# Later places in VectorE's queue for the reciprocals and x's multiplications of a linear-attention and gated-MLP kernel

## The chip, the cores and the metric

The kernel runs on one core of a Trainium2 chip. The metric is the device time of one execution in microseconds (us). A profiled execution is a single one, with its own time.

## The reference

Eight batches of eight heads (pairs of heads: 32 in all), 576 tokens each, head size 64, 128 features. In outline:

```python
proj = q_or_k @ w_phi; proj = proj - max(abs(proj))      # phi
phi = concat(exp(proj), exp(-proj))
kv = einsum('bhsf,bhsd->bhfd', k_p, v); z = sum(k_p, axis=2)
num = einsum('bhsf,bhfd->bhsd', q_p, kv)
den = einsum('bhsf,bhf->bhs', q_p, z) + 1e-06
x = (num / den) laid out as 4608 tokens x 512
out = ((x @ w_a) * (x @ w_b)) @ w_out                     # 512 -> 1536 -> 512
```

## The kernel before

**Two kinds of work side by side.** The first 630 us or so hold the attention of the 32 pairs and, interleaved with it, the first pass of the MLP over 9 blocks of 512 tokens (`moe_block`, one third of the 1536 hidden columns). After that come two more passes of the MLP over all tokens, in a form with fewer products (`later_passes`, `winograd`); no line of the change lies there. Operands are split in a high and a low part, so that most products are three matmuls.

**The steps of one pair.** `k_load` fetches and splits k and v; `features` (lines 216 to 246) projects k in two chunks of 256 tokens (`c0` = 0 and 2), and VectorE takes the largest magnitude (`m`, line 229) and subtracts it (`kd`, line 230), so each pair has two `kd` of this size; ScalarE then takes both exponentials, and VectorE makes the low part `kel`. `k_finish` makes `kvh` and `kvl`. `q_side` does the same for q and leaves unnormalized columns in `xun` and the denominators in `den`, both in DRAM (lines 381 and 382).

**Reciprocals.** `reciprocals` (lines 385 to 393) reads the denominators of a pair back as 128 rows of 9 (`r<-den`, line 389), VectorE adds EPS (line 390) and takes the reciprocal (line 391), and the result goes to `rec` in DRAM (line 392).

**x.** `x_chunk` (lines 562 to 579) loads 128 rows of `xun` (one pair's columns) for a block of 512 tokens, broadcasts that pair's `rec` over them (`rb<-rec`, line 576), and VectorE multiplies (line 578). `load_x` splits the product in `xh` and `xl` (lines 152 and 157). A block has four such chunks, c = 0 to 3, one for each pair of a batch, and every sum of line 621 needs all four. There are 36 multiplications in all. When block j is made, the last batch that it needs is `((j + 1) * 512 - 1) // 576`.

**What sets the order.** `attention_steps` lays out the steps of the pairs in turns: pair i begins at turn 5i for the first seven pairs and 4 turns apart after that, its reciprocals are at turn 13 of the pair, and the block that a finished batch allows is put into the work queue 8 turns later (`BLOCK_LAG`); the queue gives off 0.6 or 0.62 of a step in each turn. This is the order in which the program is traced. The order in each engine's queue is another one: line 1124 asks the framework to arrange every engine's queue at compile time by its own estimate of when each operand is ready, and an instruction that the estimate has ready early may be queued ahead of work that was traced before it. On the chip, each queue is then worked off in that order; an instruction that waits holds up what is queued behind it. All DMAs are issued from one queue, SyncE's (SP).

Of the kernel before, what the change touches and what calls it, by code (L numbers as in the profile page):

```python
# [13 lines left out]
ALU = mybir.AluOpType  # L14
# [4 lines left out]
P = 128  # L19
EPS = 1e-6  # L20


TURNS0, TURNS, PAIRS0 = 5, 4, 7
# [7 lines left out]
Q_TURNS, Q_STEP, QB, PB, Q32 = (4, 6, 10), 3, 2, 2, 2  # L31
# [29 lines left out]
def tile_kernel(ctx, tc, qT, km, kr, vm, vr, w_phi, w_a, w_b, w_out, out):  # L61
# [13 lines left out]
    nc = tc.nc  # L75
    B, H, _, S = qT.shape
    NPAIR = H // 2
    D, F = w_phi.shape
# [29 lines left out]
    def products(a, b):  # L108

        if len(a) == 1:  # L110
            return [(a[0], b[0])]
        return [(a[0], b[0]), (a[0], b[1]), (a[1], b[0])]
# [32 lines left out]
    def engine(step, b):  # L145
        return {"v": nc.vector, "s": nc.scalar}[ENGINES[step][min(b, 2)]]
# [7 lines left out]
    def split(hi, lo, src, eng_hi, eng_lo):  # L154

        copy(eng_hi, hi, src)
        eng_lo.tensor_tensor(lo, src, hi, op=ALU.subtract)  # L157

    def stack(hi_lo, src, eng_hi, eng_lo):

        copy(eng_hi, hi_lo, src)
        eng_lo.tensor_tensor(hi_lo[D:], src[D:], hi_lo[D:], op=ALU.subtract)

    def k_load(b, pr, a1, a2, ps, consts, st):
        vaug = consts[-1]
        u = f"{b}_{pr}"
        i = b * NPAIR + pr
        n = NFULL * P
        k32 = a1.tile([P, n], F32, tag="k32", bufs=2, name=f"k32_{u}")
        nc.sync.dma_start(k32, km[b, pr])  # L170
        if i < PLAIN_KV:
            v32 = a1.tile([P, NFULL, 2, D + 1], F32, tag="vl", bufs=2, name=f"v32_{u}")
            nc.vector.memset(v32[:, :, :, D : D + 1], 1.0)
        else:
            v32 = a1.tile([P, NFULL, 2, D], F32, tag="v32", name=f"v32_{u}")
        nc.sync.dma_start(v32[:, :, :, :D], vm[b, pr])
        yield
        st["k", b, pr] = (k32,)
        if i >= PLAIN_K:
            kh, kl = (a1.tile([P, n], F32R, tag=f"k{p}", bufs=2, name=f"k{p}_{u}") for p in "hl")  # L180
            split(kh, kl, k32, engine("k_hi", b), engine("k_lo", b))
            st["k", b, pr] = (kh, kl)
        yield
        st["v", b, pr] = (v32,)
        if i >= PLAIN_KV:
            va = vaug[pr % 2]
            vl = a1.tile([P, NFULL, 2, D + 1], F32R, tag="vl", bufs=2, name=f"vl_{u}")
            split(va[:, :, :, :D], vl[:, :, :, :D], v32, engine("v_hi", b), engine("v_lo", b))
            st["v", b, pr] = (va, vl)
        yield  # L190
# [25 lines left out]
    def features(u, i, k_, c0, n, a2, ps, consts):  # L216

        wk32, wks = consts[3:5]
        d = a2.tile([P, 4, F], F32, tag="kd", bufs=2, name=f"kd_{u}")[:, : 2 * n]
        pk = ps.tile([P, 2, 2 * F], F32, tag="att", name=f"pk_{u}")  # L220
        parts = products(k_, (wk32,) if len(k_) == 1 else wks)
        for c in range(n):
            tok = slice((c0 + c) * P, (c0 + c + 1) * P)
            for n_, (x_, w_) in enumerate(parts):
                at = dict(start=(c == n_ == 0), stop=(n_ == len(parts) - 1))
                nc.tensor.matmul(pk[:, c], x_[:, tok], w_, skip_group_check=True, **at)
        p = pk[:, :n].rearrange("p c (j f) -> p (c j) f", j=2)
        m = a2.tile([P, 4], F32, tag="m", name=f"m_{u}")
        nc.vector.tensor_reduce(out=m[:, : 2 * n], in_=p, op=ALU.max, axis=AX.X, apply_absolute_value=True)
        nc.vector.tensor_tensor(d, p, m[:, : 2 * n].unsqueeze(2).broadcast_to([P, 2 * n, F]), op=ALU.subtract)  # L230
        yield
        plain = i < PLAIN_KV
        shape = [P, 2 * n, 2, F]
        if plain:
            e = a2.tile(shape, F32, tag=f"keh{n}", bufs=n, name=f"ke_{u}")
        else:
            e = a2.tile([P, 4, 2, F], F32, tag="ke", bufs=2, name=f"ke_{u}")[:, : 2 * n]
        nc.scalar.activation(e[:, :, 0, :], d, AF.Exp)  # L238
        nc.scalar.activation(e[:, :, 1, :], d, AF.Exp, scale=-1.0)
        es = (e,)  # L240
        if not plain:
            eh = a2.tile(shape, F32R, tag=f"keh{n}", bufs=n, name=f"keh_{u}")
            el = a2.tile(shape, F32R, tag=f"kel{n}", bufs=n, name=f"kel_{u}")
            split(eh, el, e, engine("ke_hi", i // NPAIR), nc.vector)
            es = (eh, el)
        yield es
# [16 lines left out]
    def rest_chunk(b, g, a1, a2, ps, consts, st):  # L263

        gen = features(f"{b}_{g}_r", b * NPAIR + 2 * g, st["rk", b, g], 0, 1, a2, ps, consts)
        yield next(gen)
        st["re", b, g] = next(gen)
        yield
# [116 lines left out]
    def reciprocals(b, pr, a1):  # L385
        n = 2 * S // P
        hs = slice(2 * pr, 2 * pr + 2)
        r = a1.tile([P, n], F32, tag="rec", bufs=2, name=f"r_{b}_{pr}")
        nc.sync.dma_start(r, den[b][hs].rearrange("h (a n) -> (h a) n", n=n))
        nc.vector.tensor_scalar_add(r, r, EPS)  # L390
        nc.vector.reciprocal(r, r)
        nc.sync.dma_start(rec[b][hs].rearrange("h (a n) -> (h a) n", n=n), r)
        yield

    def attention_steps(pools, consts, st):

        stages, x_first = [], first_block_x()

        def plan(unit, turns):
            for t in turns:  # L400
                stages.append((t, len(stages), unit))

        for i in range(B * NPAIR):
            b, pr = divmod(i, NPAIR)
            t0 = TURNS0 * min(i, PAIRS0) + TURNS * max(i - PAIRS0, 0)
            plan(k_load(b, pr, *pools, consts, st), [t0 + t for t in LOAD_TURNS])
            if pr % 2 == 0:
                plan(rest_load(b, pr // 2, *pools, consts, st), [t0 + t for t in REST_LOAD_TURNS])
            for c0 in range(0, NFULL, 2):
                plan(k_chunks(b, pr, c0, *pools, consts, st), [t0 + K_STEP * c0 // 2 + t for t in K_TURNS])  # L410
            if pr % 2 == 0:
                plan(rest_chunk(b, pr // 2, *pools, consts, st), [t0 + t for t in REST_TURNS])
            plan(rest_add(b, pr, st), [t0 + REST_ADD_TURNS[pr % 2]])
            plan(k_finish(b, pr, *pools, consts, st), [t0 + t for t in KV_TURNS])
            plan(q_project(b, pr, *pools, consts, st), [t0 + t for t in PROJECT_TURNS])
            for j in range(2):
                plan(q_side(b, pr, j, *pools, consts, st), [t0 + Q_STEP * j + t for t in Q_TURNS])
            plan(reciprocals(b, pr, pools[0]), [t0 + Q_STEP + Q_TURNS[-1]])
            if b == 0:
                plan(x_first, [t0 + Q_STEP + Q_TURNS[-1] + X_LAG])  # L420
            if pr == NPAIR - 1:
                plan(b, [t0 + Q_STEP + Q_TURNS[-1]])
        stages.sort(key=lambda x: x[:2])
        for turn, group in itertools.groupby(stages, key=lambda x: x[0]):
            ready = None
            for _, _, unit in group:
                if isinstance(unit, int):
                    ready = unit
                else:
                    next(unit, None)  # L430
            yield turn, ready
# [130 lines left out]
    def x_chunk(j, c, pool):  # L562

        T, u = TS[0], f"0_{j}"
        x32 = pool.tile([P, T], F32, tag="x32", bufs=NCC, name=f"x32_{u}_{c}")
        rb = pool.tile([P, T], F32, tag="rb", bufs=2, name=f"rb_{u}_{c}")

        t = j * T
        while t < (j + 1) * T:
            b, s0 = divmod(t, S)  # L570
            n = min(S - s0, (j + 1) * T - t)
            src, dst = slice(s0, s0 + n), slice(t - j * T, t - j * T + n)
            nc.sync.dma_start(x32[:, dst], xun[b][c * P : (c + 1) * P, src])
            for i in range(2):
                h = 2 * c + i
                nc.sync.dma_start(rb[i * D : (i + 1) * D, dst], rec[b][h : h + 1, src].broadcast_to([D, n]))
            t += n
        nc.vector.tensor_tensor(x32, x32, rb, op=ALU.mult)  # L578
        return x32

    def load_x(j, pool):
# [6 lines left out]
    def first_block_x():  # L588

        for x_ in load_x(0, xpool):  # L590
            first_x.append(x_)
            yield
# [404 lines left out]
    with ExitStack() as c:  # L997
        pools = attention_pools(c)
# [129 lines left out]
```

## Time and profile before

| | |
|---|---|
| median of 3 runs | 1244.07 us (1243.14 to 1244.48) |
| the profiled execution, its own time | 1244.96 us |
| its span from first to last instruction | 1243.2 us |
| PE busy | 1190.3 us (96%), x6237 |
| PE weight loads | 985.4 us (79%) |
| VectorE (DVE) busy | 1043.5 us (84%) |
| ScalarE (ACT) busy | 726.4 us (58%) |
| mean granted clock of TensorE | 0.990 |

The span is 1.8 us shorter than the execution's own time. PE is TensorE's matmuls, DVE is VectorE, ACT is ScalarE, POOL is GpSimd. Ends of matmuls are modelled, so small pauses between them are inside the busy time. [...]

### The profile page before, as it was taken

The page shows a single profiled execution, that of the slowest core. Times are in us where ns is not written, and L with a number is a line of the kernel's source. Part 1 is how long each engine was busy: PE and PEld are TensorE (multiplying, and loading weights), DVE is VectorE, ACT ScalarE, POOL GpSimd, SP SyncE. Part 2 cuts the span into 40 slices and gives each one's busy share as a digit, 9 for nine tenths or more (in the row PEclk, how much of TensorE's full clock was granted, in tenths as well). Part 3 has the DMA queues.
Part 4 walks back from the last instruction along what each step waited for, and adds up shares of the span by engine and source line. Part 5 has one row for each costly group of instructions (what it writes and reads, how often), then busy time and mean ns, then how long its engine had stood idle before and what let it go on. Part 6 is the DMA issues. An engine that isn't in the chain of part 4 may idle for free.

```text
span 1243.2 us, 18172 instructions
## 1 busy us (share of the span) xinstructions
PE 1190.3 (96%) x6237; PEld 985.4 (79%) x6237; DVE 1043.5 (84%) x1742; ACT 726.4 (58%) x1376; POOL 154.3 (12%) x68
## 2 busy tenths in 40 slices
PE   7979989999999999999999999999999999999998
PEld 4546778888888887888778888888888888888887
DVE  7989969998989899898589866889888688888686
ACT  5677778878888878788444443344444243434332
POOL 3321313222123133132100000000000000000000
PEclk9989999999999999999999999999999999999999
DMA  6764344353544445343283331647489714242312
GB/s 197 197 200 130 110 132 125 111 160 111 157 134 138 145 119 150 115 127 104 76 262 109 119 109 45 223 167 245 154 293 392 251 53 152 69 153 68 127 62 92
DMA packets 130173, 182.84 MB, mean 147 GB/s; under 512 B 35936, under 2 KB 64992, under 8 KB 130080
## 3 DMA queue, kind: packets, MB, share of 16 engines
q1 hardware_dynamic: 130080, 181.67, 46.5%
q8 instruction: 49, 0.80, 0.3%
q14 instruction: 44, 0.36, 0.1%
HBM read 123.06 MB, written 58.56 MB: 146 GB/s over the span
## 4 chain that ended last, share of the span: by engine, by line
PE 40%; DVE 7%; DMA 3%; ACT 1%; issue 1%; SPq 0%; DVEq 0%; ACTq 0%
PE po L928 7%; PE pba L716 7%; PE paa L716 7%; PE pac L716 3%; PE poa L821 3%; PE pbc L716 3%; PE po L642 3%; PE pab L716 2%; PE pb L621 2%; PE pbb L716 2%; PE pa L621 2%; DVE o L825 1%; DMA x<-xnorm 1%; DVE hl_s L157 1%; DVE top L777 1%
## 5 line engine op out<-in xcount | busy, mean ns | idle before, releaser
L359 POOL PARTITION_ALL_REDUCE mb<-p x64 | 154.2, 2437 | 439.8 <-ACT p L350 325.5
L157 DVE TENSOR_TENSOR qel<-qe,qeh 128x1152 fp32r<-128x1152 f32 x54 | 75.8, 1405 | 3.1 <-ACT qeh L150 3.0
L363 ACT ACTIVATE qe<-p 128x576 f32<-128x576 f32 x64 | 43.9, 687 | 45.2 <-DVE p L360 41.6
L578 DVE TENSOR_TENSOR x<-x,rb 128x512 f32<-128x512 f32 x36 | 31.3, 869 | 40.7 <-DMA rb<-rec 35.9
L157 DVE TENSOR_TENSOR kel<-ke,keh 128x1024 fp32r<-128x1024 f32 x50 | 62.3, 1246 | 3.7 <-ACT keh L150 3.5
L621 PE MATMUL pa<-xh,w_a_h 128*128 128x512 f32 x144 | 58.4, 405 | 6.5 <-DVE xh L152 4.9
L150 ACT CAST qeh<-qe 128x1152 fp32r<-128x1152 f32 x54 | 63.0, 1166 | 0.0
L642 PE MATMUL po<-hh,w_o_h 128*128 128x512 f32 x144 | 57.4, 408 | 5.5 <-DVE h L626 4.5
L621 PE MATMUL pb<-xh,w_b_h 128*128 128x512 f32 x144 | 58.4, 406 | 3.8 <-ACT h L625 1.4
L621 PE MATMUL pa<-xl,w_a_h 128*128 128x512 f32 x144 | 57.8, 401 | 4.2 <-DVE xl L157 4.2
L282 PE MATMUL kvps<-keh,vaug 128*65 128x256 f32 x200 | 56.3, 282 | 2.8 <-DVE kvl L312 2.8
L238 ACT ACTIVATE ke<-kd 128x512 f32<-128x512 f32 x64 | 40.8, 637 | 29.9 <-DVE kd L230 28.3
L642 PE MATMUL po<-hl,w_o_h 128*128 128x512 f32 x144 | 58.0, 404 | 0.0
L621 PE MATMUL pb<-xl,w_b_h 128*128 128x512 f32 x144 | 57.9, 402 | 0.0
L642 PE MATMUL po<-hh,w_o_l 128*128 128x512 f32 x144 | 57.7, 402 | 0.0
L621 PE MATMUL pb<-xh,w_b_l 128*128 128x512 f32 x144 | 57.6, 400 | 0.0
L621 PE MATMUL pa<-xh,w_a_l 128*128 128x512 f32 x144 | 57.3, 398 | 0.0
L928 PE MATMUL po<-hl,w_o_h 128*128 128x512 f32 x144 | 56.4, 392 | 0.3 <-DVE hl L157 0.3
L928 PE MATMUL po<-hh,w_o_l 128*128 128x512 f32 x144 | 56.1, 389 | 0.0
L282 PE MATMUL kvps<-keh,vl 128*64 128x256 f32 x200 | 55.8, 279 | 0.0
L282 PE MATMUL kvps<-kel,vaug 128*65 128x256 f32 x200 | 55.8, 279 | 0.0
L150 ACT CAST keh<-ke 128x1024 fp32r<-128x1024 f32 x50 | 52.5, 1049 | 4.2 <-PE kvps L282 4.0
(338 smaller groups left out, 3877.1 us busy)
## 6 DMA issues: line engine op xcount, KB each, us to landing
x<-xnorm SPq DMA_DIRECT2D x32, 512.0 KB
o<-part SPq DMA_DIRECT2D x61, 256.0 KB
q<-in_qT SPq DMA_DIRECT2D x108, 144.0 KB
xun<-xn SPq DMA_DIRECT2D x64, 144.0 KB
xnorm<-x SPq DMA_DIRECT2D x36, 256.0 KB
part<-o SPq DMA_DIRECT2D x18, 512.0 KB
part<-o SPq DMA_DIRECT2D x36, 256.0 KB
k<-in_km SPq DMA_DIRECT2D x32, 256.0 KB
```

The source lines that it names most:

```text
L150: eng.copy(dst, src)
L157: eng_lo.tensor_tensor(lo, src, hi, op=ALU.subtract)
L238: nc.scalar.activation(e[:, :, 0, :], d, AF.Exp)
L282: nc.tensor.matmul(st["kv_ps", b, pr][:width, j], v_[:, j, :width], e_[:, j], start=(left == NFULL and j == 0 and n_ == 0), stop=(left == ...
L359: nc.gpsimd.partition_all_reduce(mb, p32, P, bass_isa.ReduceOp.absmax)
L363: nc.scalar.activation(e[:, 0], p32, AF.Exp)
L578: nc.vector.tensor_tensor(x32, x32, rb, op=ALU.mult)
L621: nc.tensor.matmul(acc, w[:, cc * P : (cc + 1) * P], x, start=(k == 0), stop=(k == 3 * NCC - 1))
L642: nc.tensor.matmul(acc, w[:, cc * P : (cc + 1) * P], h, start=(k == 0), stop=(k == 3 * NFS[p] - 1))
L716: nc.tensor.matmul(accs[to][i], w_, x_, skip_group_check=True, **at)
L821: nc.tensor.matmul(accs[to][m], w_, x_, skip_group_check=True, **flags)
L928: nc.tensor.matmul(acc[key], w[:, cc * P : (cc + 1) * P], h[:, tok], skip_group_check=True, **n_)
```

## The change

A dictionary keeps, for each pair, the two `kd` instructions of line 230. The add of a pair from the eighth on (i >= 7) is queued on VectorE behind the second `kd` of the pair three later; x's multiplication of such a pair is queued behind the first `kd` of the pair four later. `tc.issue_after` fixes the order within one engine's queue and adds no wait. Where that pair does not exist (the last batch), the multiplication is kept behind the VectorE instruction traced just before it (`tc.keep_in_program_order`); the adds of the last three pairs get no such place. The add, the reciprocal and the store of `rec` are traced two turns after the load of the denominators instead of in the same turn, for all pairs.

```diff
+    behind = {}
+
+    def placed(i, c0, op):
+
+        if i >= PAIRS0 and (i + c0[0], c0[1]) in behind:
+            with tc.issue_after(behind[i + c0[0], c0[1]]):
+                return op()
+        return op()
+
@@ features
-        nc.vector.tensor_tensor(d, p, m[:, : 2 * n].unsqueeze(2).broadcast_to([P, 2 * n, F]), op=ALU.subtract)
+        kd = nc.vector.tensor_tensor(d, p, m[:, : 2 * n].unsqueeze(2).broadcast_to([P, 2 * n, F]), op=ALU.subtract)
+        if n == 2:
+            behind[i, c0] = kd.ins
@@ reciprocals
         nc.sync.dma_start(r, den[b][hs].rearrange("h (a n) -> (h a) n", n=n))
-        nc.vector.tensor_scalar_add(r, r, EPS)
+        yield
+        placed(b * NPAIR + pr, (3, 2), lambda: nc.vector.tensor_scalar_add(r, r, EPS))
         nc.vector.reciprocal(r, r)
@@ attention_steps
-            plan(reciprocals(b, pr, pools[0]), [t0 + Q_STEP + Q_TURNS[-1]])
+            plan(reciprocals(b, pr, pools[0]), [t0 + Q_STEP + Q_TURNS[-1] + t for t in (0, 2)])
@@ x_chunk
-        nc.vector.tensor_tensor(x32, x32, rb, op=ALU.mult)
+        multiply = lambda: nc.vector.tensor_tensor(x32, x32, rb, op=ALU.mult)
+        pair = ((j + 1) * T - 1) // S * NPAIR + c
+        if pair + 4 < B * NPAIR:
+            placed(pair, (4, 0), multiply)
+        else:
+            tc.keep_in_program_order(multiply())
```

## Rows read from the trace of the kernel before

**Rows 1.** Busy time by stretch: us from:to, length, busy us of each engine, granted clock.

```profile
180.00:190.00 10.00, 7.42 (x33) 5.94 (x32) 6.46 (x11) 4.84 (x11) 0.20 (x1) 0.83 0.34 105
...
490.00:505.00 15.00, 11.65 (x60) 9.54 (x59) 12.79 (x18) 11.92 (x25) 5.15 (x2) 0.89 0.53 167
...
616.00:626.00 10.00, 6.97 (x17) 5.19 (x18) 5.74 (x13) 1.67 (x3) 0.00 (x0) 0.66 0.64 188
626.00:650.00 24.00, 22.59 (x96) 17.59 (x95) 21.84 (x50) 12.80 (x29) 0.00 (x0) 1.00 0.84 275
sum 490.00, PE 469.07 PEld 404.88 DVE 425.58 ACT 378.72 POOL 108.98; mean PE 46.91 PEld 40.49 DVE 42.56 ACT 37.87 POOL 10.90
```

**Rows 2.** PE's waits, 160 to 632 us: total us, times, longest us.

```profile
PE pa L621 <- DVE xl L157: 4.2, 3, 2.6
PE pa L621 <- DVE xh L152: 4.0, 4, 2.6
PE po L642 <- DVE h L626: 3.0, 1, 3.0
PE kvps L282 <- DVE kvl L312: 2.8, 3, 1.3
```

**Rows 3.** Line 578, 160 to 600 us: VectorE's idle time before it (us, times).

```profile
  DMA rb<-rec: 20.9, 14
```

**Rows 4.** Line 390, 160 to 600 us, the same columns.

```profile
  DMA r<-den: 10.7, 9
```

**Rows 5.** VectorE's timeline at the end of the attention: start us, us, instruction, [idle before].

```profile
609.01 0.22 DVE L391 RECIPROCAL r<-r 128x9 f32<-128x9 f32 x1
...
614.68 0.69 DVE L578 TENSOR_TENSOR x<-x,rb 128x512 f32<-128x512 f32 x1 [4.90 <-DMA rb<-rec]
...
618.23 0.68 DVE L626 TENSOR_TENSOR h<-pb,h 128x512 f32<-128x512 f32 x1
```

**Rows 6.** VectorE's timeline: second kd of pair 19, first kd of pair 20.

```profile
354.12 0.68 DVE L230 TENSOR_TENSOR kd<-pk,m 128x512 f32<-128x512 f32 x1
...
360.64 0.68 DVE L230 TENSOR_TENSOR kd<-pk,m 128x512 f32<-128x512 f32 x1
```

**Rows 7.** SyncE's queue, 160 to 600 us: waits, total us, times, longest us.

```profile
SPq L392 <- DVE r L391: 29.1, 18, 3.0
```

**Rows 8.** VectorE's timeline, blocks 1 to 6: chunk 3's multiplication, then first kd four pairs later.

```profile
183.47 0.69 DVE L578 TENSOR_TENSOR x<-x,rb 128x512 f32<-128x512 f32 x1 [4.75 <-DMA rb<-rec]
...
196.01 0.68 DVE L230 TENSOR_TENSOR kd<-pk,m 128x512 f32<-128x512 f32 x1
...
266.06 1.31 DVE L578 TENSOR_TENSOR x<-x,rb 128x512 f32<-128x512 f32 x1 [1.06 <-DMA rb<-rec]
...
272.86 0.69 DVE L230 TENSOR_TENSOR kd<-pk,m 128x512 f32<-128x512 f32 x1
...
341.18 0.81 DVE L578 TENSOR_TENSOR x<-x,rb 128x512 f32<-128x512 f32 x1 [0.92 <-DMA rb<-rec]
...
344.22 0.68 DVE L230 TENSOR_TENSOR kd<-pk,m 128x512 f32<-128x512 f32 x1
...
414.02 0.69 DVE L578 TENSOR_TENSOR x<-x,rb 128x512 f32<-128x512 f32 x1 [1.02 <-DMA rb<-rec]
...
425.03 0.68 DVE L230 TENSOR_TENSOR kd<-pk,m 128x512 f32<-128x512 f32 x1
...
492.83 0.69 DVE L578 TENSOR_TENSOR x<-x,rb 128x512 f32<-128x512 f32 x1 [0.68 <-DMA rb<-rec]
...
494.88 0.68 DVE L230 TENSOR_TENSOR kd<-pk,m 128x512 f32<-128x512 f32 x1
...
567.43 0.69 DVE L578 TENSOR_TENSOR x<-x,rb 128x512 f32<-128x512 f32 x1 [1.50 <-DMA rb<-rec]
...
577.49 0.68 DVE L230 TENSOR_TENSOR kd<-pk,m 128x512 f32<-128x512 f32 x1
```

**Rows 9.** The chain of waits in order of time: start us, us, what.

```profile
631.43 2.80 PE pa L621 x12
```

## The prediction

> **What bounds the kernel now.** I read the profile in this order. First the busy times by stretch, from 160 us (about where the places of the change begin to act) to 650 us (the end of the attention): PE is busy 469.1 of 490 us, DVE 425.6 [rows 1]. So PE has about 21 us of visible pauses here, and no more than these, with what a lower clock costs, can be won while PE's work stays the same; after 650 us the change has nothing. Second, PE's own waits from 160 to 632 us [rows 2]: nearly all of the time stands against DVE, and most of it against two of its products, xh and xl of line 621 (8.2 us in seven waits), a single wait of 3.0 us for h, and three for kvl (2.8 us). Third, what DVE itself waited for in these places: in 160 to 600 us it stood 20.9 us at x's multiplication until the broadcast of rec had landed [rows 3] and 10.7 us at the add until the denominators had [rows 4], 31.6 us together. While it stands, the steps that make PE's operands are queued behind the waiting instruction.
>
> The granted clock ties the two together. Three stretches lie below full clock: 180 to 190 us at 0.83, 490 to 505 us at 0.89, 616 to 626 us at 0.66 [rows 1]. Each holds one of the three long PE stops: 2.6 us for xh, 2.6 us for xl, 3.0 us for h [rows 2]. In the first, the multiplication of block 1's last chunk started at 183.47 us after DVE had stood 4.75 us [rows 8]. In the last, DVE stood 4.90 us before a multiplication at 614.68 us, and h, which PE needed, came behind it at 618.23 us [rows 5]. [...]
>
> **The change part by part.** The sum is made against the profiled execution's 1244.96 us, which is 0.9 us above the median of the runs.
>
> *No instruction is added.* The counts of DVE, PE and DMA instructions stay. The new order edges lie within DVE's queue, so there is no new semaphore wait; they cost nothing by themselves.
>
> *Adds and reciprocals behind the second kd three pairs later, multiplications behind the first kd four pairs later.* The data then has at least the distance between these two kd to come: the tightest that I found from pair 7 on is 354.12 to 360.64 us, 6.5 us [rows 6]. A reciprocal at 609.01 us was followed by its multiplication at 614.68 us [rows 5], 5.7 us for the store, the broadcast and the wait in SP's queue. 6.5 is above 5.7, so the waits of rows 3 and 4 should nearly vanish. The SP queue: the store of rec holds SP until the reciprocal is done, 29.1 us in 18 waits [rows 7]. The store and the broadcasts move with the reciprocal, so SP waits for it neither more nor less as long as the arranged order moves too; behind them stand loads of k, v and q, which are issued some turns ahead of their use. I take 0.
>
> What PE gets back:
> - the end: block 7's and 8's multiplications are pinned behind what was traced before them, so h of block 6 no longer stands behind them. The stop of 3.0 us goes, and the clock with it: 10 us at 0.66 lose 3.4 us. 6.4 us.
> - block 1: 2.6 us, and 10 us at 0.83, 1.7 us. 4.3 us.
> - block 5: 2.6 us, and 15 us at 0.89, 1.65 us. 4.25 us.
> - the other five waits for xh and xl: 8.2 - 5.2 = 3.0 us.
> - kvl: it is merely late in DVE's queue. Between 0 and 2.8 us; I take the middle, 1.4, since only some of these waits have a DVE stop close ahead of them.
>
> Together 19.35 us.
>
> What it costs. The last chunk of a block now comes later, and no sum of line 621 can end without it. Work passed over, less the multiplication's own wait that goes, is kd start - multiplication start - wait [rows 8]: block 1: 12.54 - 4.75 = 7.79; block 2: 6.80 - 1.06 = 5.74; block 3: 3.04 - 0.92 = 2.12; block 4: 11.01 - 1.02 = 9.99; block 5: 2.05 - 0.68 = 1.37; block 6: 10.06 - 1.50 = 8.56. Sum 35.6 us, in which PE has only attention and the three earlier chunks. Lower end: 0, attention fills it all (it is ready sooner when DVE does not stand). Upper end: the MLP's whole share of PE is lost. Twelve matmuls of 512 columns take 2.80 us [rows 9], so a block's 144 take 33.6 us; from pair 11's kd at 196.01 to pair 27's at 494.88 us [rows 8] are four batches, 74.7 us each; share 0.45, 16.0 us. I take 8.2 us, because the nearest row is what waiting for xh and xl costs at these same starts today [rows 2]: the next late operand is again the last chunk's xh and xl, only at another place in the queue.
>
> *Pinned multiplications of block 8.* Its four multiplications of 0.69 us, 2.8 us in all, move from gaps to just ahead of their casts, where DVE is busy 21.84 of 24 us [rows 1]. Between 0 and 2.8 us; I take 1.0, nearer to 0, as the 48 output matmuls of block 7 (11.2 us at the pace of rows 9) stand on PE meanwhile. Below 0 there is nothing: they gain no time by going later.
>
> *The two turns for the first seven pairs and the last three*, which get no place. The add there may be queued a little later or earlier. I take 0, with two mean waits of rows 4 (10.7 / 9 = 1.2 us) to either side, 2.4 us.
>
> Sum: -19.35 + 8.2 + 1.0 = -10.15 us. 1244.96 - 10.15 = 1234.8 us; less the 0.9 us by which the profiled execution lies over the median, **1234 us**. With the bounds: all costs at 0, kvl whole and 2.4 us to the good, 1244.07 - 20.75 - 2.4 = 1221 us; all costs at their upper ends, kvl at 0, 1244.07 - 17.95 + 16.0 + 2.8 + 2.4 = 1247 us. About what can be told from no change in this kernel is 0.2%, 2.5 us.
>
> **The rivals.**
>
> *DVE is the bound, and all that it waited comes off.* For it: it is busy 425.6 of 490 us and stood another 31.6 us in 160 to 600 us [rows 3, 4], so it had little left. Against it: PE has only 21 us of visible pauses to give [rows 1], and its work does not shrink. It would give 1244.07 - 31.6 = 1212 us. [...] Chance 0.08.
>
> *Slower: the blocks starve PE.* The place is chunk 3 of blocks 1 to 6. The first kd four pairs later is a worse place than the wait was: the stops for xh and xl do not go, they move with the chunk. Then the gains left are the end and kvl, 6.4 + 1.4 = 7.8 us, less 1.0 for block 8. It turns where more than 6.8 us of the 35.6, 19%, finds no attention work. At 0.35 of it, 12.5 us, the time is 1244.07 - 6.8 + 12.5 = 1250 us; at the full 0.45 and with two starts at the lower clock (1.7 us each, as now) 1257 us. For it: the operands of attention come from the same DVE, 87% busy, and block 4's and block 6's chunks come 10.0 and 8.6 us later. Against it: today's starts are waited for too, and cost 8.2 us in all. Chance 0.20.
>
> *No change that can be told.* Two ways lead here. The places fix an order, not a distance: if attention quickens and the two kd come closer than the 5.7 us of the chain, part of the waits returns. Or the whole order of PE is arranged anew and small pauses open elsewhere, by as much as the waits give back. 1242 to 1246 us. Chance 0.16.
>
> **How the numbers follow.** The forecast has 0.56, the rivals 0.08, 0.20 and 0.16. Faster by over 0.2%: forecast and the first rival, 0.64. Within: 0.16. Slower: 0.20. The forecast's own range is 1227 to 1241 us. The range of 8 in 10 runs from 1222 us, where nearly all of the gain comes at no cost, to 1248 us, the forecast's upper bound and the nearer part of the slower rival; left out are the first rival and the farther part of the second.
>
> **What would show it.** In the profile after: DVE's idle time before lines 578 and 390 in 160 to 600 us falls from 31.6 us to under 6 us; the stretch around the end of block 6 has no stop for h and no clock below 1; PE's waits for xh and xl stand near 8 us, without a stop above 2 us; chunk 3's multiplications come right behind a kd. If idle time before these lines stays over 15 us, the spacing was misjudged. If it goes and the time does not fall, PE's waits will show it: a sum for xh and xl above 15 us is the slower rival; PE pauses gone and the attention's end 25 us or more earlier would be the first.

## The result and the profile after

The changed kernel takes 1227.59 us (median of 4 runs, 1223.45 to 1227.88), the kernel before 1244.28 us beside it (4 runs). The ratio, which is formed from all runs and not from the two medians, is 0.9855, with a 95% interval of 0.9829 to 0.9881. In the medians it is 16.7 us, 1.3%, faster. The forecast was 10.15 us faster, 1234 us; 1227.59 us lies at the lower edge of its own range of 1227 to 1241 us. The profiled execution after took 1227.31 us, its span is 1225.4 us, 17.8 us shorter than before.

The order of reading is that of the prediction. First the busy times by stretch of the changed kernel (columns as in [rows 1]), the three stretches that had lain below full clock and then 160 to 630 us:

```profile
180.00:190.00 10.00, 10.00 (x74) 9.16 (x72) 8.97 (x17) 9.67 (x21) 3.73 (x2) 1.00 0.44 129
...
490.00:505.00 15.00, 14.53 (x87) 12.19 (x86) 12.22 (x18) 13.41 (x25) 4.26 (x2) 1.00 0.37 99
...
616.00:626.00 10.00, 10.00 (x43) 8.07 (x44) 9.43 (x21) 4.76 (x11) 0.00 (x0) 1.00 1.08 335
```

```profile
160.00:630.00 470.00, 461.61 (x2838) 401.89 (x2837) 414.71 (x645) 376.79 (x720) 104.83 (x46) 1.00 0.47 137
```

and the same stretch of the kernel before:

```profile
160.00:630.00 470.00, 450.48 (x2748) 390.52 (x2747) 406.10 (x616) 367.87 (x702) 108.98 (x45) 0.99 0.44 131
```

PE's pauses in this stretch went from 19.5 us to 8.4 us, 11.1 us less, and 90 more matmuls fit in. The three stretches with a granted clock of 0.83, 0.89 and 0.66, which lost 1.7, 1.65 and 3.4 us by an estimate from [rows 1] (length times what the clock lacks of 1), are at full clock, 1.00. 11.1 + 6.75 = 17.9 us is as much as the whole difference, in the stretch and of the kind that the prediction named.

The row of 180 to 190 us flatters, though: block 1's stop did not go, it moved behind this row. A wider stretch shows it, in the kernel before, in the changed one, and in a kernel with the changed one's queues (x from pair 8, below):

```profile
180.00:215.00 35.00, 32.42 (x187) 27.76 (x186) 30.67 (x47) 27.12 (x53) 9.41 (x4) 0.95 0.41 122
```

```profile
180.00:215.00 35.00, 30.37 (x213) 26.55 (x211) 33.78 (x51) 29.97 (x59) 9.61 (x4) 1.00 0.47 135
```

```profile
180.00:215.00 35.00, 31.53 (x212) 27.60 (x211) 33.91 (x52) 30.09 (x59) 9.62 (x4) 0.95 0.44 123
```

PE pauses 2.6 us there in the kernel before and 4.6 us in the changed one, and in the repetition the lower clock is back as well, 0.95 as in the kernel before. What was won in pauses lies behind it: 215 to 630 us has 14.9 us of them before and 1.7 us after.

A second look at the same sum is the end of the MLP's first pass on PE, the last matmul with the 512 columns of block 8 before the first of the second pass. In the kernel before and in the changed one (timeline of PE: start us, us, instruction):

```profile
700.18 0.39 PE L642 MATMUL po<-hh,w_o_l 128*128 128x512 f32 x1
```

```profile
681.16 0.40 PE L659 MATMUL po<-hh,w_o_l 128*128 128x512 f32 x1
```

19.0 us earlier; what follows takes 1225.4 - 681.2 = 544.2 us instead of 1243.2 - 700.2 = 543.0 us, 1.2 us more. That 17.9 us meets the difference of the spans, 17.8 us, is in part chance, because this execution of the changed kernel was already 1.9 us behind before 160 us (first kd of pair 9, before and after):

```profile
155.31 0.68 DVE L230 TENSOR_TENSOR kd<-pk,m 128x512 f32<-128x512 f32 x1
```

```profile
157.16 0.68 DVE L239 TENSOR_TENSOR kd<-pk,m 128x512 f32<-128x512 f32 x1
```

So the changed kernel loses 1.9 us up to there, wins 17.9 us in the stretch and another 3.0 us up to the end of the first pass, and loses 1.2 us behind it.

Then PE's own waits, 160 to 632 us, which answer to [rows 2]:

```profile
PE pk L235 <- DVE kd L239: 1.7, 1, 1.7
PE pa L638 <- ACT o L661: 1.5, 1, 1.5
PE pn L390 <- ACT kvh L319: 1.3, 1, 1.3
...
PE pa L638 <- DVE xl L157: 0.8, 1, 0.8
PE pa L638 <- DVE xh L152: 0.5, 1, 0.5
PE pb L638 <- DVE h L643: 0.5, 1, 0.5
```

The waits for xh and xl fell from 8.2 to 1.3 us, those for kvl and the long one for h are gone. And VectorE's idle time before the multiplication (now line 590) and the add (now line 402) in 160 to 600 us, which answers to [rows 3, 4]:

```profile
  DMA rb<-rec: 6.2, 6
```

```profile
  DMA r<-den: 1.1, 2
```

31.6 us became 7.3 us. How a last chunk stands now shows in VectorE's timeline at block 3 (start us, us, instruction, idle time before it): the second kd of pair 18, the reciprocal of pair 15, the first kd of pair 19 and the multiplication.

```profile
326.90 0.68 DVE L239 TENSOR_TENSOR kd<-pk,m 128x512 f32<-128x512 f32 x1
...
329.24 0.21 DVE L403 RECIPROCAL r<-r 128x9 f32<-128x9 f32 x1
...
332.11 0.68 DVE L239 TENSOR_TENSOR kd<-pk,m 128x512 f32<-128x512 f32 x1
...
334.22 0.97 DVE L590 TENSOR_TENSOR x<-x,rb 128x512 f32<-128x512 f32 x1 [1.41 <-DMA rb<-rec]
```

The multiplication comes right behind the kd, as it should (a clearing of 0.06 us stands between them), and here its broadcast was still 1.4 us late. The two kd are 5.2 us apart, and the reciprocal starts 2.3 us behind the first of them.

### The profile page after: what moved, and what is told of

Its sections match the earlier page's. It is cut to its first block, busy times and chain, and to the rows that moved or that the text cites. A ratio compares the mean times of both kernels' runs of the same rounds, so it can differ in the third digit from the quotient of the medians.

```text
span 1225.4 us, 18164 instructions
## 1 busy us (share of the span) xinstructions
PE 1183.1 (97%) x6237; PEld 982.3 (80%) x6237; DVE 1038.5 (85%) x1742; ACT 726.0 (59%) x1376; POOL 149.7 (12%) x68
## 4 chain that ended last, share of the span: by engine, by line
PE 69%; DVE 15%; DMA 9%; ACT 3%; issue 3%; SPq 1%; DVEq 0%; ACTq 0%
PE kvps L293 7%; PE pb L638 7%; PE po L945 7%; PE pa L638 7%; PE pba L733 6%; PE paa L733 6%; PE po L659 6%; PE pn L390 6%; PE poa L838 3%; PE pac L733 3%; PE pbc L733 3%; PE pk L235 2%; PE pq L360 2%; PE pab L733 2%; PE pbb L733 2%
## 5 line engine op out<-in xcount | busy, mean ns | idle before, releaser
L370 POOL PARTITION_ALL_REDUCE mb<-p x64 | 149.5, 2366 | 426.9 <-ACT p L361 320.6
L157 DVE TENSOR_TENSOR kel<-ke,keh 128x1024 fp32r<-128x1024 f32 x50 | 65.2, 1304 | 6.8 <-ACT keh L150 6.4
L355 DVE TENSOR_TENSOR qs<-q,qs 64x576 fp32r<-64x576 f32 x54 | 54.1, 1007 | 2.0 <-ACT qs L150 0.4
L391 ACT COPY xn<-pn 65x288 f32<-65x288 f32 x128 | 47.6, 398 | 12.6 <-PE pn L390 12.2
```

Source lines behind the costliest of these rows:

```text
L355: nc.vector.tensor_tensor(qs[j][D:], q32[j][D:], qs[j][D:], op=ALU.subtract)
L370: nc.gpsimd.partition_all_reduce(mb, p32, P, bass_isa.ReduceOp.absmax)
L391: nc.scalar.copy(xn[: D + 1, tok], pn[: D + 1, :HALF])
```

## The experiments

Four theories were put against each other. A: the gain is what PE lost when VectorE stood at a DMA. B: any rearranged order would have done. C: the two places only work together. D (formed on the way): it is enough that a block's sums are queued later on PE, with slack behind their last chunk. One limit holds for all runs: each edit that changed VectorE's order changed PE's, too, so no run takes VectorE's waits away and leaves all else as it was. All ratios are to the kernel before on the same chip, whose medians in these series were 1244 to 1248 us; so ratios are compared, not times.

**One part at a time.** Only x's multiplications (the reciprocals as before):

```diff
-        yield
-        placed(b * NPAIR + pr, (3, 2), lambda: nc.vector.tensor_scalar_add(r, r, EPS))
+        nc.vector.tensor_scalar_add(r, r, EPS)
...
-            plan(reciprocals(b, pr, pools[0]), [t0 + Q_STEP + Q_TURNS[-1] + t for t in (0, 2)])
+            plan(reciprocals(b, pr, pools[0]), [t0 + Q_STEP + Q_TURNS[-1]])
```

> Only x's multiplications get their new places; the reciprocals stay as before. Theory A (the gain is the PE stops and the lower clock that came out of VectorE standing at a DMA): the waits for the broadcast of rec (20.9 us in 160 to 600 us) fall under 6 us, the waits for the denominators (10.7 us) stay; most of the gain, 1229 to 1234 us. Theory B (any rearranged order would have done it, the waits don't matter): no relation between the waits left and the time; 1228 to 1246 us with the waits anywhere. Theory C (the two places only work together): 1240 us or more.

Measured: 0.9883 (0.9853 to 0.9914), 1230.95 us. The waits for the broadcast fell to 3.1 us, those for the denominators stayed at 11.7 us, as theory A had it. Theory C, which wanted 1240 us or more, falls.

Only the reciprocals (two turns and their place):

```diff
-        if pair + 4 < B * NPAIR:
-            placed(pair, (4, 0), multiply)
-        else:
-            tc.keep_in_program_order(multiply())
+        multiply()
```

> Only the reciprocals get their new place and the two turns; x's multiplications are free. Theory A: the waits for the denominators fall under 3 us, those for the broadcast stay near 21 us or rise, since the chain behind the reciprocal is as long as before; PE's stops at the end and at blocks 1 and 5 stay in kind; 1238 to 1244 us. Theory B: as likely 1228 as 1246 us.

Measured: 0.9922 (0.9894 to 0.9950), 1235.87 us, below the 1238 to 1244 us that theory A gave; the waits for the denominators, which it wanted under 3 us, are 7.0 us. VectorE's waits for DMAs before the two lines, 160 to 600 us, are still 24.9 us (total, times, longest):

```profile
DVE x L590 <- DMA rb<-rec: 17.9, 11, 3.2
...
DVE r L402 <- DMA r<-den: 7.0, 3, 3.3
```

but PE's waits for xh and xl are 0.8 + 0.5 = 1.3 us, as in the changed kernel. This raised theory D: the reciprocal's later place makes x later in the arranging, too, so that the sums of a block stand behind more attention work on PE.

Only the last batch's pinned multiplications:

```diff
         pair = ((j + 1) * T - 1) // S * NPAIR + c
         if pair + 4 < B * NPAIR:
-            placed(pair, (4, 0), multiply)
+            multiply()
         else:
             tc.keep_in_program_order(multiply())
```

(with the reciprocals as before.)

> Only the last batch's multiplications are pinned behind what was traced before them; all else as before. Theory A: the 3.0 us stop for h of block 6 and the low clock behind it go, 6.4 us: about 1238 us, and nothing changes before 560 us. Theory B: 1244 us, or anything.

Measured: 0.9993 (0.9976 to 1.0010): not told from no change, where theory A expected about 1238 us. Yet the stop for h is gone and the stretch around it is at full clock, 1.00 where the kernel before had 0.76 (busy times of this kernel, then of the kernel before):

```profile
616.00:630.00 14.00, 13.70 (x58) 10.45 (x57) 8.19 (x16) 2.91 (x5) 0.00 (x0) 1.00 0.64 191
```

```profile
616.00:630.00 14.00, 10.97 (x34) 8.41 (x35) 8.10 (x17) 3.61 (x6) 0.00 (x0) 0.76 0.76 238
```

Its first pass ends at 695.1 us, 5.1 us earlier (timeline of PE):

```profile
695.08 0.39 PE L658 MATMUL po<-hh,w_o_l 128*128 128x512 f32 x1
```

while its span, 1240.0 us, is 3.2 us shorter: the rest takes 544.9 us instead of 543.0 us. So part of the gain at the end is given back behind the first pass. The other traces say that this comes of the pinned multiplications: from the same matmul to the end, the five kernels whose last batch is free take 542.0 to 543.0 us, the nine in which it is pinned 543.4 to 548.1 us.

The changed kernel without the pinned multiplications:

```diff
         else:
-            tc.keep_in_program_order(multiply())
+            multiply()
```

> The changed kernel without the pinned multiplications of the last batch (they are free again). Theory A: the stop for h comes back at the end of block 6, 3 to 7 us: 1231 to 1234 us. If the end is no term of its own, it stays at 1227 to 1228 us.

Measured: 0.9881 (0.9854 to 0.9908), 1231.01 us. A stop comes back, for hl instead of h:

```profile
PE po L659 <- DVE hl L157: 2.5, 1, 2.5
PE pb L638 <- DVE h L643: 1.9, 1, 1.9
```

0.9881 - 0.9855 = 0.0026, 3.2 us: the lower edge of what was expected, and not clear of the noise, as the two intervals overlap. The parts alone give 0.0117 (with the end) and 0.0078, together 0.0195, and both at once 0.0145: they overlap.

**Is it the order as such?** The two turns alone, with no place for anything:

```diff
-        placed(b * NPAIR + pr, (3, 2), lambda: nc.vector.tensor_scalar_add(r, r, EPS))
+        nc.vector.tensor_scalar_add(r, r, EPS)
...
-        if pair + 4 < B * NPAIR:
-            placed(pair, (4, 0), multiply)
-        else:
-            tc.keep_in_program_order(multiply())
+        multiply()
```

> Add, reciprocal and store are traced two turns later, and nothing gets a place. Theory A (the places do it, by taking VectorE's waits away): about 1244 us, the waits of both kinds stay near 30 us. Theory D (formed after the first four runs: it is enough that the planner thinks x later, so that it queues the sums of a block on TensorE with slack behind their last chunk): part or all of what the reciprocals' place alone gave, 1236 to 1241 us.

Measured: 0.9999 (0.9983 to 1.0015). The traces of this kernel and the kernel before hold the same instructions by name and shape in the same order on every engine, but for two short neighbours on VectorE before 60 us that change places; so the two turns do nothing by themselves, and this is a repetition of the kernel before.

Only the casts xh and xl behind the first kd four pairs later; the adds and the multiplications as before (`behind` and `placed` are those of the change):

```diff
-            split(xh, xl, x32, nc.vector, nc.vector)
+            pair = ((j + 1) * TS[0] - 1) // S * NPAIR + c
+            placed(pair, (4, 0), lambda: split(xh, xl, x32, nc.vector, nc.vector))
```

> Reciprocals and multiplications are as in the kernel before, with their waits; only the two casts of each chunk (xh and xl) go behind the first kd four pairs later, so that the sums of a block are queued later on TensorE while VectorE goes on standing at the DMAs. Theory A (VectorE's waits are what costs): the waits stay near 31 us and the time near before, 1241 to 1246 us. Theory D (it is the slack of the sums behind their last chunk): TensorE's waits for xh and xl fall from 8.2 us under 2 us, and the time to that of the reciprocals' place alone, 1234 to 1238 us.

Measured: 0.9992 (0.9974 to 1.0010): nothing. VectorE's waits before the two lines were 36.4 us:

```profile
DVE x L589 <- DMA rb<-rec: 21.8, 13, 4.7
DVE r L401 <- DMA r<-den: 14.6, 9, 2.9
```

and PE's waits, 160 to 632 us:

```profile
PE kvps L293 <- DVE kvl L323: 5.2, 6, 2.6
PE pq L360 <- DVE kd L239: 4.2, 3, 3.1
PE po L654 <- DVE hl L157: 2.6, 2, 2.3
PE po L654 <- DVE h L638: 2.3, 3, 1.8
...
PE pa L633 <- DVE xl L157: 0.6, 1, 0.6
```

The waits for x are gone, as theory D wants, but kvl rose from 2.8 to 5.2 us, kd from 0.6 to 4.2 us, and hl with 2.6 us is new; h has 3.8 us as before 3.9 us. Slack in the sums only moves the stop to the next operand that VectorE makes late. Theory D falls; B too, for this order is new on PE and brings nothing.

**Distance and lateness.** x's multiplications behind the same kd as the pair's add, so that there is an order but no distance:

```diff
-            placed(pair, (4, 0), multiply)
+            placed(pair, (3, 2), multiply)
```

> x's multiplications go behind the second kd three pairs later, the same instruction that the pair's add goes behind: an order, but no distance. Theory A: the waits for the broadcast come back, 15 us or more in 160 to 600 us, and with them TensorE's stops: 1234 to 1242 us. Theory D: the waits come back, but the sums keep their slack on TensorE: 1228 to 1236 us.

Measured: 0.9907 (0.9880 to 0.9933), 1235.39 us; waits of 14.7 + 5.1 = 19.8 us. 12.5 us more of VectorE's waits than in the changed kernel go with 0.0052, 6.5 us. The order without the distance already gives 0.0093 of the 0.0145; the reciprocals' place alone gave 0.0078 of it.

One pair later, and half a pair later:

```diff
-            placed(pair, (4, 0), multiply)
+            placed(pair, (5, 0), multiply)
```

> x's multiplications go behind the first kd five pairs later instead of four (for the last chunk of block 6 there is no such pair; it is free). The last chunk of a block comes about 17 us later still. The slower rival of the prediction (blocks starve TensorE) at a larger dose: at a share of 0.2 to 0.45 of 17 us in five blocks, 17 to 38 us, 1245 to 1265 us. Theory A: waits are gone in either case, and attention fills TensorE: 1226 to 1232 us. Theory D: the same, 1226 to 1232 us.

```diff
-            placed(pair, (4, 0), multiply)
+            placed(pair, (4, 2), multiply)
```

> x's multiplications go behind the second kd four pairs later instead of the first, about 9 us later. Between the changed kernel and one pair later, which was some 8 us slower: if lateness costs in proportion, 1229 to 1233 us; if the distance is still short in the changed kernel (6 us of waits are left in 160 to 600 us), as fast or faster, 1225 to 1228 us.

Measured: one pair later 0.9911 (0.9879 to 0.9943), 1235.21 us, with 0.8 + 0.8 us of waits; half a pair later 0.9875 (0.9847 to 0.9904), 1232.92 us, with 2.1 us. Half a pair later cannot be told from the changed kernel. One pair later has hardly a wait and is 0.0056, 7 us, slower than the changed kernel, where theory A expected 1226 to 1232 us and the slower rival 1245 us or more. PE waits there for attention's own operands:

```profile
PE pk L235 <- DVE kd L239: 2.7, 2, 1.7
PE pn L390 <- ACT kvh L319: 2.6, 1, 2.6
```

PE's pauses in 160 to 630 us are 12.0 us instead of 8.4 us. So lateness costs, but not as the slower rival had it: its stops were to be for xh and xl, and these waits are 0.4 us.

**Two tries at less.** Pair 7 free of its place:

```diff
-            placed(pair, (4, 0), multiply)
+            placed(pair, (4, 0), multiply) if pair > PAIRS0 else multiply()
```

> As the changed kernel, but pair 7, the last chunk of block 1, is free: the stops that the changed kernel has at 192 to 208 us around this block (1.9, 0.6, 1.5, 1.0 us) should go or change. If this chunk comes too late in the changed kernel, 1223 to 1226 us; if the wait of 4.7 us returns with the low clock, 1227 to 1230 us.

Measured: 0.9835 (0.9804 to 0.9866), 1226.46 us. In the traces the queues are the same as the changed kernel's on every engine, so this is a repetition of it: 0.9855 and 0.9835 show how far two series of one program lie apart. This chunk does come 13 us later than in the kernel before, and PE pauses 2 us more around it; what another place for it would give stays open.

Places for the first seven pairs, too:

```diff
-        if i >= PAIRS0 and (i + c0[0], c0[1]) in behind:
+        if i < PAIRS0:
+            c0 = (2, 2) if c0 == (3, 2) else (3, 0)
+        if (i + c0[0], c0[1]) in behind:
...
-DECODE_TURN, X_LAG, BLOCK_LAG = 2, 2, 8
+DECODE_TURN, X_LAG, BLOCK_LAG = 2, 3, 8
```

> The changed kernel, and the first seven pairs get places too: their adds behind the second kd two pairs later, their multiplications behind the first kd three pairs later (the first block's x is traced one turn later for it). Theory A: the 10 us of waits before 160 us go; TensorE's low clock before 110 us (13.6 us at half in the changed kernel, so 6.8 us lost) shrinks; 1221 to 1226 us. If the first 160 us hang on something else (loads, plain matmuls): 1226 to 1230 us. If the first block comes too late: above 1230 us.

Measured: 0.9901 (0.9871 to 0.9932), 1236.06 us, slower than the changed kernel and in the range that was given for a first block that comes too late. VectorE's waits from 160 us on are 13.1 us again, but that is not where most of it was lost: in 160 to 630 us PE is busy 462.41 us at a granted clock of 1.00, against 461.61 us, also at 1.00, in the changed kernel. Its first pass ends 2.9 us later (684.04 us), and what follows takes another 3.9 us more (548.1 us). Why was not taken apart.

The first three chunks half a pair later, the last one as in the changed kernel:

```diff
-            placed(pair, (4, 0), multiply)
+            placed(pair, (4, 0 if c == NCC - 1 else 2), multiply)
```

> The changed kernel, with the first three chunks of a block behind the second kd four pairs later, and the last chunk, on which the block's sums hang, behind the first as in the changed kernel. If the waits that are left cost as those that went did (6.2 us for the broadcast in 160 to 600 us, most of them before the first three chunks), and only the last chunk's lateness costs: waits under 3 us, a ratio to the kernel before of 0.981 to 0.985, 1222 to 1227 us. If the first three chunks' lateness costs too, a ratio of 0.986 to 0.989, as with all four half a pair later.

Measured: 0.9872 (0.9852 to 0.9891), 1230.21 us. The waits fell to 1.7 + 0.3 = 2.0 us, and the time did not follow; 0.986 to 0.989 was expected if the first three chunks' lateness costs, too, but the ratio cannot be told from the changed kernel's. PE's busy time in 160 to 630 us is 462.24 us against 461.61 us:

```profile
160.00:630.00 470.00, 462.24 (x2828) 401.86 (x2826) 417.77 (x644) 376.84 (x721) 108.01 (x45) 1.00 0.47 137
```

**All in one table** (VectorE's waits before the add and the multiplication in 160 to 600 us):

| kernel | waits, us | PE's waits for xh and xl, us | ratio |
|---|---|---|---|
| before | 31.6 | 8.2 | 1 |
| two turns alone (same queues as before) | 31.4 | 8.7 | 0.9999 |
| end alone | 30.8 | 6.9 | 0.9993 |
| casts alone | 36.4 | 0.6 | 0.9992 |
| reciprocals alone | 24.9 | 1.3 | 0.9922 |
| no distance | 19.8 | 1.5 | 0.9907 |
| x alone | 14.8 | 0 | 0.9883 |
| changed, end free | 13.5 | 1.3 | 0.9881 |
| **changed** | 7.3 | 1.3 | 0.9855 |
| the same queues again | 6.4 | 0.5 | 0.9835 |
| last chunk first | 2.0 | 0.5 | 0.9872 |
| half a pair later | 2.1 | 4.8 | 0.9875 |
| one pair later | 1.6 | 0.4 | 0.9911 |
| early pairs | 13.1 | 2.0 | 0.9901 |

Down to the changed kernel the ratio falls with VectorE's waits, and not with the waits for x alone. Below some 7 us of waits nothing more was won, and one pair later shows what lateness costs. Two kernels stand off the line. The early pairs lost at other places, as said. The reciprocals alone have 6.7 us fewer waits and gave 0.0078, 9.7 us: PE's pauses in 160 to 630 us are 16.9 us there, 2.6 us fewer than before, and the granted clock over this stretch is 1.00 where the kernel before had 0.99. Why so little time at the lower clock goes with the waits that are left is open.

## Why the prediction was right, and which terms were not

*What bounds.* Right. TensorE's pauses and its lower clock in 160 to 630 us are what came back, 11.1 and 6.75 us. What the lower clock was shows in the trace of the kernel before: behind the 3.0 us stop for h the granted clock in 620 to 624 us was 0.50, and matmuls of 128x512 started 0.43 us apart there, where they started 0.23 us apart at 1.00 in 612 to 614 us. The first rival, VectorE as the bound, is out: in the last-chunk-first run the last 5.3 us of its waits (7.3 to 2.0 us) brought nothing, and in 160 to 630 us of the changed kernel PE is busy 98%, VectorE 88%.

*The distance of 6.5 us against a chain of 5.7 us.* Nearly right: 7.3 us of waits are left where under 6 us were expected. The comparison had two faults, and block 3 above shows both. The 5.7 us count from the reciprocal, the 6.5 us from the kd ahead of it, 2.3 us earlier there; and the two kd came closer than in the kernel before, 5.2 us, as the rival that ends in no change had named. So 1.4 us of waiting was left. That the distance takes these waits away, not the order, the no-distance run shows (19.8 us of waits); most of the gain in time, 0.0093 of 0.0145, comes without it.

*The stops for xh and xl at blocks 1 and 5, the other five, and kvl.* Right for block 5, the other five and kvl: 8.2 us became 1.3 us, kvl's 2.8 us went whole where half was taken, and block 5's low clock went, too (490 to 505 us, 0.89 to 1.00). Wrong for block 1, taken at 4.3 us: PE's pauses in 180 to 215 us rose from 2.6 to 4.6 us, now mostly for kd and kvh, and of the 1.7 us of clock the repetition gives nothing back (0.95 in 180 to 215 us, as before).

*The end, 6.4 us, and block 8's pinned multiplications, 1.0 us.* The mechanism was right, the balance too large. The stop and the low clock behind it go (616 to 630 us, 0.76 to 1.00 with the end alone), and with the end alone the first pass ends 5.1 us earlier; but the ratio is then 0.9993, and in the changed kernel the end is worth 0.0026, 3.2 us. What follows the first pass takes 1.2 us (changed kernel) to 1.9 us (end alone) longer, and over all traces the nine pinned kernels take on average 2.8 us more there than the five others: the 1.0 us taken for block 8 was at the low end of what was measured.

*The cost of the late last chunk, 8.2 us.* This is the term that failed. It rested on "the last chunk of a block now comes later", by 35.6 us in six blocks, and that holds for block 1 alone. Its multiplication starts at 196.68 us instead of 183.47; those of blocks 2 to 6 start at 266.05, 334.22, 414.01, 484.59 and 553.89 us, where [rows 8] has 266.06, 341.18, 414.02, 492.83 and 567.43. Blocks 1, 2 and 6 of the changed kernel, with the kd ahead of block 6's:

```profile
196.68 0.68 DVE L590 TENSOR_TENSOR x<-x,rb 128x512 f32<-128x512 f32 x1
...
266.05 0.69 DVE L590 TENSOR_TENSOR x<-x,rb 128x512 f32<-128x512 f32 x1 [0.20 <-DMA rb<-rec]
...
551.92 0.69 DVE L239 TENSOR_TENSOR kd<-pk,m 128x512 f32<-128x512 f32 x1
...
553.89 1.70 DVE L590 TENSOR_TENSOR x<-x,rb 128x512 f32<-128x512 f32 x1 [0.48 <-DMA rb<-rec]
```

The prediction left the kd behind which the chunk is queued at its old time, but it comes earlier itself: 551.92 us instead of 577.49 for block 6, 332.11 instead of 344.22 for block 3. That VectorE no longer stands ahead of it fits this; how much the new arrangement of the queues adds was not taken apart. So a later place in the queue was not a later time, and the only block that did come later is the one whose stop did not go. The reason given for the size, "the next late operand is again the last chunk's xh and xl, only at another place in the queue", did not hold either: those waits measured 1.3 us where the prediction's own sign for it was near 8 us. With 1.3 in the place of 8.2 the sum is -19.35 + 1.3 + 1.0 = -17.05 us, against 17.65 us between the two profiled executions. That it fits so well is luck: it counts block 1's stop as gone, and leaves out the other half of kvl and most of 2.8 us of small waits for kvT, h and kd, which went as well.

*The slower rival.* At four pairs its condition hardly arose, as only block 1's chunk came later. Where chunks do come later, lateness has a price, but a far lower one. Going one pair later, the last chunks of blocks 1 to 6 came at 204.47, 276.03, 352.98, 430.15, 499.90 and 560.96 us instead of 196.68, 266.05, 334.22, 414.01, 484.59 and 553.89 us, 75 us in sum, and it cost 7 us, 0.09 of it, where the rival needed over 0.19. The places without distance and one pair later are slower than four pairs; half a pair later is not told from it.

*The two turns for the other pairs.* Right at 0: by themselves they change the order of two short instructions and no time.

*SP's queue, taken at 0.* No run tests it alone. Its waits for the reciprocal at the store fell from 29.1 us [rows 7] to 15.2 us and those for ScalarE's xn rose from 10.2 to 37.0 us, so its order moved, too; of PE's waits above none names a DMA.

## What to carry to other kernels

What a VectorE instruction that waited for a DMA cost here was what stood queued behind it, so look at the engine that is held up and not at the idle time of the one that waits: 24 us less waiting on VectorE came with 11 us less of TensorE's pauses and, by the estimate above, 7 us of clock. Give such an instruction a distance, behind work that runs longer than its transfers take, rather than only an order (7.3 us of waits against 19.8 us here), and count both from the same instruction; and try other places to both sides, because the order alone left 6.5 us and one pair further lost 7 us. Before costing the lateness, ask whether a later place is a later time at all, since what it is queued behind moves, too; before trusting a term at the end, see what it pushes into the next stage.

## What the runs showed of the hardware that was not expected

The length of the stretch at the lower clock behind a stop differed between two executions with the same queues. The kernel with the two turns has the same queues as the kernel before; around the same stop, a 2.6 us wait of PE for xl in both, its granted clock in 490 to 505 us is 0.77 where the kernel before had 0.89 [rows 1], 1.8 us more lost, and in 616 to 630 us it is 0.88 where that had 0.76:

```profile
490.00:505.00 15.00, 11.51 (x50) 9.14 (x49) 12.37 (x17) 11.83 (x25) 5.29 (x2) 0.77 0.58 171
...
616.00:630.00 14.00, 10.79 (x40) 8.03 (x39) 8.46 (x17) 3.13 (x6) 0.00 (x0) 0.88 0.74 224
```

So the 3.4 us at the end, a term read from one execution's clock, differed by 1.7 us, half of it, between these two.
